# Scores of the global rows: eight heads of a batch as one block of eight tiles, in four PSUM banks

## The chip, the cores and the metric

The kernel runs on one core of one Trainium2 chip. The metric is device time in microseconds of one execution; the kernel before takes 904.69 us (median of three runs).

## What is computed

Two steps: attention of 8 batches with 8 heads each, and then a feed-forward layer on its output. Each head has 512 local rows and 32 global rows of 64 elements. A global row attends to all 544 keys; a local row attends to the 32 global keys and to the local keys at most 32 positions away.

```python
s_g = scale * np.matmul(q_g, k_all.transpose(0, 1, 3, 2))      # k_all: 32 global + 512 local keys
out_g = np.matmul(sm(s_g), v_all)
s_ll = np.where(mask, scale * np.matmul(q_l, k_l.transpose(0, 1, 3, 2)), -1000000000.0)
s_l = np.concatenate([s_lg, s_ll], axis=-1)                    # s_lg: local rows, global keys
out_l = np.matmul(sm(s_l), np.concatenate([v_g, v_l], axis=2))
attn_out = np.concatenate([out_g, out_l], axis=2)
x = attn_out.transpose(0, 2, 1, 3).reshape(B * S, H * D)       # 4352 x 512
h = x @ w_in                                                   # 512 x 2048
g = h * erf(np.maximum(h, 0.0) + np.log1p(np.exp(-np.abs(h))))
out = g @ w_out
```

## The kernel before

**Local rows.** The keys of a head lie in 24 blocks of 32, some of them twice, so that each of 16 windows of 32 rows finds its keys in 128 columns. `attention` (line 451) does one head: q and k come for a pair of heads (64 partitions each), va and vb (the values, one row of them all ones, which gives the softmax sum) for each head. A *run of window scores* (tile `s`) is a pair of heads: 32 small matmuls in the program, 64 rows by 32 columns of the array each, 128 columns wide; in fp32 each is two matmuls in the trace. VectorE masks them and takes the maximum (`sm`, `mx`), ScalarE takes the exponentials, TensorE transposes (`t`), a copy brings them to SBUF (`pt`), and TensorE multiplies with the values (`o`: 128 rows by 32 columns of the array). VectorE divides by the sum (`rs`, `xn`), and the result goes to DRAM by way of a transposed tile (`xT`).

**Global rows.** Four heads are a group. `global_scores` (line 675) computes their scores with four small matmuls of 480 columns into one PSUM bank (`ga`) and four of 64 columns into another (`gb`); head hh uses rows 64 x (hh mod 2) and columns 32 x hh of the array. Then come maximum (`gm`, `gn`), exponentials into the one tile `pg`, six transposes (`gt`), and the values (`go`: 24 matmuls in the program, 48 in the trace), which read the va tiles of the four heads. `global_rows` (line 753) normalizes, and a matmul with a selection matrix (`gx`) brings two heads into place. From batch 5 on (`GSJOIN`) a group's scores are one step with a run of window scores, from batch 6 on (`GOJOIN`) `go` is one step with a pair of `o`.

**Feed-forward.** `x` is split into two parts (`xh`, `xl`), as the weights are, and every product is three matmuls. During the attention the first three eighths of the hidden layer are computed (`h`, the gate, then `op`) for the batches that are done, between the attention's steps. Behind the attention the other five eighths follow, with fewer products by sums of blocks (`pa` to `pd`). TensorE's work is thus of three kinds: full matmuls (`h`, `op`, the transposes, `gx`), score tiles (`s`, `ga`, `gb`) and value tiles (`o`, `go`).

**What sets the order.** Each step is put on a list with `add` (line 131): the engines that may run it, a time to run, a key and what it reads and writes. `schedule` (line 173) plays the list through in the host program and always takes the ready step with the lowest key, if its buffers are free. The keys come from the table of numbers at the top (lines 28 to 78: `HKEYS`, `HOFF` and so on). `NEAR` is how far a step of TensorE's present kind may come ahead of its key; `EVADE`, `CROWD` and `STRETCH` hold back steps of many small instructions. The instructions of each engine then run in that order; all loads and stores are issued on SyncE's queue. `psum_a` has six banks for `s`, `t`, `o`, `ga`, `gb`, `gt`, `go`, `gx` and `op`, a second pool has two for `h`. Until the first `h`, matmuls on constants (`spare`) fill TensorE's planned gaps.

Of the kernel before, what the change touches and what calls it, by code (L numbers as in the profile page):

```python
# [29 lines left out]
CROWD, STRETCH, EVADE = 254, 4.013, 0.302  # L30
# [5 lines left out]
HKEYS = ((0, -4.808), (11, -0.938), (22, 0.485), (64, 33.202))  # L36
STEP, GKEY = 0.082, -0.59
QLEAD, VLEAD, RLEAD, XLEAD = 0.802, -1.384, -3.274, 5.136
GOFF, POFF = 6.111, 3.439
WIN, WOUT = (1.692, -0.833, -2.539), (5.372, 5.751, 6.572)  # L40
BIASED, AG = 28, 3
SHARED = (-99.0, 10.395)
TPAIR = 3.723
KEEP, KSTEP, FIRST = 25.717, 1.786, (18.732, 17.811)
CVO = (54.239, 54.957, 78.914, 61.099, 65.318)
QLEAD2, XDEL, SLOTS = 2.849, -2.014, 11
GATE1, GATE2, PROJ1, PROJ2 = (18.529, 22.625, 24.302), (22.055, 24.328, 43.477), 16.064, 32.464
# [19 lines left out]
WLEAD = 2.131  # L67
LATER, GFIRST = 8, (-3.104, -5.093)
HOFF = (-0.552, -0.319, 0.052, -0.145, -0.077, -0.13, 0.035, -0.016, -0.005, -0.046, 0.01, -0.049, -0.013, 1.49, 2.105, -0.254, 0.767, 0.207, -0.21, 0.858, 0.388, -0.382, 1.584, -2.479, 0.129, -0.149, -0.895, 0.741, 3.078, -0.931, 2.609, 4.711)
XOFF = (-1.743, 3.531, 4.132, 6.479, -2.355, 1.289, 6.274, -1.424, -2.0)  # L70
UOFF = (2.693, -0.229, -0.111, -0.488, 10.393, -2.037, 0.678, -8.495, 2.152)
GFF = (-0.013, 0.75, -1.267, 1.697, -1.821, -1.427, -1.715, -1.652, -1.918)
PFF = (0.156, 0.123, 0.319, 0.471, 0.761, 2.958, 1.452, 0.32, -1.362)
KQ = (2.677, 1.804, -0.704, -0.365, 4.117, -1.317, 9.687, 0.998, 2.585, -6.754)
NORMAL = 1.125 * 2.0**-15
STRAIGHT, XLATE = True, -4.089
# [264 lines left out]
def kernel(  # L341
# [68 lines left out]
    cs = attn.tile([P, 512 + P + 64 + 2], F32, name="cs")  # L410
# [40 lines left out]
    def attention(b, h, key):  # L451
        nm = f"{b}_{h}"
        p, r0 = h // 2, (h % 2) * D
        if h % 2 == 0:
            st["q"] = Q = abuf([P, SQ], f"q_{nm}", "q", 2)
            st["k"] = K = abuf([P, NENT * WB], f"k_{nm}", "k", 2)
            load(key - QLEAD, Q, qT[b, p], 278)
            load(key - QLEAD, K, kE[b, p], 393)
# [7 lines left out]
        st["va", h % 4] = VA  # L466

        biased = NH * b + h < BIASED
        if h % 2 == 0:
# [16 lines left out]
            if h % 4 == 2 and b >= GSJOIN:  # L486
                GA, GB, more = global_scores(b, h // 4, [st["qk", 0], (Q, K)])
                G0[b, h // 4] = GA, GB
# [5 lines left out]
                add({"PE": 1.9}, key, joint, [*st["qk", 0], Q, K], [*SS, GA, GB, GTURN], heat=3136, ins=160, mode="S")  # L494
# [110 lines left out]
        if h % 4 == 3 and not joined:  # L605
# [147 lines left out]
    def global_rows(b, j, O, key):  # L753
        nm = f"{b}_{j}"
        RS = abuf([P, 1], f"gr_{nm}", "gr", 2)

        def norm():
            dve.tensor_scalar(RS.ap, O.ap[:, D : D + 1], 1e-9, None, op0=ALU.add)
            dve.reciprocal(RS.ap, RS.ap)
            dve.tensor_scalar(HALF.ap, half, RS.ap, None, op0=ALU.mult)  # L760
# [642 lines left out]
def _layout(q_l, k_l, v_l, q_g, k_g, v_g, moe_w_in, moe_w_out):  # L1403
# [60 lines left out]
```

## Time and profile before

| | |
|---|---|
| median of 3 runs | 904.69 us (904.61 to 908.22) |
| profiled execution: time | 904.46 us |
| profiled execution: span | 902.7 us |
| mean granted clock of TensorE | 0.996 of full speed |
| instructions in the span | 22276 |
| TensorE busy | 885.5 us |
| VectorE busy | 682.9 us |
| ScalarE busy | 543.7 us |
| GpSimd busy | 12.1 us |
| moved by DMA | 188.22 MB, mean 209 GB/s |

The span is the time from the first to the last instruction of the profiled execution; its own time is a little longer. TensorE has two rows in the profile: PE is its matmuls, PEld its loads of weights, which run beside them. A matmul's row lasts longer than the step from one matmul to the next, because matmuls overlap in the array; what a run costs is read from its start to the start of the run behind it.

### The profile page before, as it was taken

How to read it: one execution, taken by the hardware profiler on the slowest of the kernel's cores; microseconds unless marked ns; L12 is line 12 of the kernel's file. 1: busy time of each engine (PE TensorE's matmuls, PEld its weight loads, DVE VectorE, ACT ScalarE, POOL GpSimd, SP SyncE). 2: the span in 40 equal slices, each digit the busy share in tenths (PEclk: the TensorE clock that was granted, in tenths of full speed). 3: DMA queues.
4: the chain of work that ended last, by engine and by line, in shares of the span. 5: the costliest groups of instructions: out<-in, count | busy, mean ns of one | idle time of the engine just before them, and what ended most of it. 6: DMA issues, size and time to landing. Idle time of an engine off the chain costs nothing.

```text
span 902.7 us, 22276 instructions
## 1 busy us (share of the span) xinstructions
PE 885.5 (98%) x8807; PEld 721.2 (80%) x8807; DVE 682.9 (76%) x1821; ACT 543.7 (60%) x912; POOL 12.1 (1%) x13
## 2 busy tenths in 40 slices
PE   8789999999999999999999999999999999999998
PEld 5567787888878888888888888888888888888886
DVE  6798999969997899987898686487736965465553
ACT  5667977736673796657645583565517571553850
POOL 0002100000000000000000000000000000000000
PEclk9899999999999999999999999999999999999999
DMA  9878886888769958377499836644366426436013
GB/s 337 305 231 286 263 266 211 242 269 278 241 217 299 318 177 292 125 273 274 168 297 369 278 95 192 225 117 129 110 171 211 150 86 195 139 108 213 19 48 117
DMA packets 110016, 188.22 MB, mean 209 GB/s; under 512 B 15576, under 2 KB 39384, under 8 KB 109912
## 3 DMA queue, kind: packets, MB, share of 16 engines
q1 hardware_dynamic: 109912, 186.79, 63.7%
q8 instruction: 70, 1.15, 0.5%
q14 instruction: 34, 0.28, 0.1%
HBM read 145.59 MB, written 41.16 MB: 207 GB/s over the span
## 4 chain that ended last, share of the span: by engine, by line
PE 89%; DMA 5%; DVE 2%; ACT 2%; issue 1%; SPq 1%; DVEq 0%; ACTq 0%
PE op L379 40%; PE h L379 13%; PE pd L379 6%; PE pc L379 6%; PE pa L379 6%; PE o L379 3%; PE pb L379 3%; PE s L379 3%; PE t L380 3%; PE h_g L379 2%; PE ga L379 1%; DMA vb<-in_vB_dram 1%; PE go L379 1%; SPq L383 1%; PE gt L380 1%
## 5 line engine op out<-in xcount | busy, mean ns | idle before, releaser
L379 PE MATMUL op<-wouth,gh 128*128 128x512 f32 x544 | 215.8, 397 | 0.0
L379 PE MATMUL op<-wouth,gl 128*128 128x512 f32 x544 | 212.1, 390 | 0.0
L379 PE MATMUL op<-woutl,gh 128*128 128x512 f32 x544 | 212.0, 390 | 0.0
L382 ACT ACT_TABLE_LOAD x108 | 138.6, 1283 | 2.6 <-PEq L1451 0.7
L379 PEld LDWEIGHTS op<-wouth,gl 128*128 128x128 f32 x544 | 102.1, 188 | 21.8
L379 PEld LDWEIGHTS op<-wouth,gh 128*128 128x128 f32 x544 | 102.2, 188 | 21.5 <-issue 0.6
L379 PEld LDWEIGHTS op<-woutl,gh 128*128 128x128 f32 x544 | 102.3, 188 | 19.5
L381 ACT ACTIVATE gh<-sp 128x512 fp32r<-128x512 f32 x65 | 40.2, 629 | 104.9 <-PE op L379 88.8
L391 DVE TENSOR_TENSOR gl<-sp,gh 128x512 fp32r<-128x512 f32 x134 | 90.4, 689 | 12.8 <-PE op L379 9.3
L379 PE MATMUL h<-xh,winh 128*128 128x512 f32 (+1 forms) x216 | 85.2, 395 | 0.0
L379 PE MATMUL h<-xh,winl 128*128 128x512 f32 (+1 forms) x216 | 81.9, 379 | 0.0
L379 PE MATMUL h<-xl,winh 128*128 128x512 f32 (+1 forms) x216 | 81.7, 378 | 0.0
L381 ACT ACTIVATE sp<-sp 128x512 f32<-128x512 f32 x136 | 75.9, 622 | 0.5
L391 DVE CUSTOM_DVE_ANT_0 sm<-s,cs 128x128 f32<-128x128 f32 x256 | 57.6, 285 | 15.4 <-PE s L379 8.3
L391 DVE CAST gh<-sp 128x512 fp32r<-128x512 f32 x71 | 29.2, 422 | 36.0 <-PE op L379 35.8
L379 PE MATMUL pd<-xh_T,wq 128*128 128x512 f32 x160 | 55.6, 389 | 0.0
L379 PE MATMUL pa<-xh_B,wq 128*128 128x512 f32 x160 | 55.6, 389 | 0.0
L379 PEld LDWEIGHTS h<-xh,winh 128*128 128x128 f32 x216 | 40.6, 188 | 9.8 <-issue 2.2
L379 PEld LDWEIGHTS h<-xh,winl 128*128 128x128 f32 x216 | 40.6, 188 | 8.0
L391 DVE TENSOR_TENSOR pair<-u,pc 128x512 f32<-128x512 f32 x40 | 27.4, 685 | 24.8 <-PE pc L379 24.5
L379 PEld LDWEIGHTS h<-xl,winh 128*128 128x128 f32 x216 | 40.7, 189 | 6.7
L379 PE MATMUL o<-vb,pt 128*32 128x65 f32 x1280 | 37.7, 221 | 7.0 <-issue 5.1
(160 smaller groups left out, 1640.3 us busy)
## 6 DMA issues: line engine op xcount, KB each, us to landing
wq<-wq SPq DMA_DIRECT2D x140, 256.0 KB, 3.0
vb<-in_vB_dram SPq DMA_DIRECT2D x64, 325.0 KB, 5.6
rx<-xsc SPq DMA_DIRECT2D x30, 512.0 KB, 5.5
va<-in_vA_dram SPq DMA_DIRECT2D x64, 195.0 KB, 5.4
k<-in_kE_dram SPq DMA_DIRECT2D x32, 384.0 KB, 5.0
wq<-part SPq DMA_DIRECT2D x35, 256.0 KB, 5.0
q<-in_qT_dram SPq DMA_DIRECT2D x32, 272.0 KB, 4.5
part<-os SPq DMA_DIRECT2D x34, 256.0 KB, 4.6
```

The lines of the kernel that those rows point to most:

```text
L379: pe = lambda n, *a, **k: pinned(nc.tensor.matmul(n, *a, **k))
L380: tr = lambda *a, **k: pinned(nc.tensor.transpose(*a, **k))
L381: act = lambda *a, **k: pinned(nc.scalar.activation(*a, **k))
L382: table = lambda name: pinned(nc.scalar.preload_act_table_set(name))
L383: dma = lambda *a, **k: pinned(nc.sync.dma_start(*a, **k))
L391: return lambda *a, **k: pinned(f(*a, **k))
```

## The change

From batch 1 on (`WHOLE`) `whole_scores` takes the place of two calls of `global_scores`. It issues the scores of all eight heads as one *block*: the eight `ga` matmuls in the order half 0, half 1 for each of the four column places, then the eight `gb` matmuls. The second half takes its heads with their neighbours swapped (`n ^ j`), so that it uses the other 64 rows at each column place. The block has two `ga` and two `gb` banks. In batches 1 to 4 it is a step of its own behind head 7, in batches 5 to 7 one step with the window scores of heads 6 and 7. The softmax and the values of each half are as before, but both come behind the block; `go` is no longer one step with `o`. The swap is taken back by a third column of the `half` mask. q and k tiles are held in rings of four, va in one of seven, vb in one of three (the plan counts on two of them, as before). The numbers that set the order are all different.

```diff
-CROWD, STRETCH, EVADE = 254, 4.013, 0.302
+CROWD, STRETCH, EVADE = 254, 4.013, 0.92
...
-HKEYS = ((0, -4.808), (11, -0.938), (22, 0.485), (64, 33.202))
+HKEYS = ((0, -4.835), (11, -0.96), (22, 0.654), (64, 33.085))
...
-MORE = {"vb": 2}
+MORE = {"vb": 1}
...
-NEAR = 7.126
+NEAR = 0.48
...
+WHOLE, KBUFS, QBUFS, VBUFS = 1, 4, 4, 7
+G2KEY = 0.438
...
-EARLY |= {"k_0_6": ("k3", 0), "q_0_6": ("q3", 0)}
...
-            st["q"] = Q = abuf([P, SQ], f"q_{nm}", "q", 2)
-            st["k"] = K = abuf([P, NENT * WB], f"k_{nm}", "k", 2)
+            st["q"] = Q = abuf([P, SQ], f"q_{nm}", "q", QBUFS)
+            st["k"] = K = abuf([P, NENT * WB], f"k_{nm}", "k", KBUFS)
...
-        VA = abuf([P, NENT // 4, D + 1], f"va_{nm}", "va", 5)
-        VB = abuf([P, NWIN - 6, D + 1], f"vb_{nm}", "vb", 4)
+        VA = abuf([P, NENT // 4, D + 1], f"va_{nm}", "va", VBUFS)
+        VB = abuf([P, NWIN - 6, D + 1], f"vb_{nm}", "vb", 3)
...
-            if h % 4 == 2 and b >= GSJOIN:
-                GA, GB, more = global_scores(b, h // 4, [st["qk", 0], (Q, K)])
-                G0[b, h // 4] = GA, GB
+            if h == 6 and b >= GSJOIN:
+                GA, more = whole_scores(b, [st["qk", n] for n in range(4)])
...
-                add({"PE": 1.9}, key, joint, [*st["qk", 0], Q, K], [*SS, GA, GB, GTURN], heat=3136, ins=160, mode="S")
+                add({"PE": 2.05}, key, joint, [x for n in range(4) for x in st["qk", n]], [*SS, *GA, GTURN], heat=4200, ins=192, mode="S")
...
-        if h % 4 == 3 and b >= GOJOIN:
+        if h % 4 == 3 and WHOLE > b >= GOJOIN:
...
-        if h % 4 == 3 and not joined:
+        if b >= WHOLE:
+            if h == 7:
+                if b < GSJOIN:
+                    GA, scores = whole_scores(b, [st["qk", n] for n in range(4)])
+                    add({"PE": 1.05}, key + GKEY, scores, [x for n in range(4) for x in st["qk", n]], [*GA, GTURN], heat=2176, ins=64, mode="S")
+                for j in range(2):
+                    attention_global(b, j, [st["va", 4 * j + (i ^ j)] for i in range(4)], None, key + GKEY + G2KEY * j)
+        elif h % 4 == 3 and not joined:
...
+    def whole_scores(b, qk):
+        GA = [psum_a([P, 480], f"ga_{b}_{j}") for j in range(2)]
+        GB = [psum_a([P, 64], f"gb_{b}_{j}") for j in range(2)]
+        G0[b, 0], G0[b, 1] = zip(GA, GB)
+
+        def scores():
+            for T, k0 in ((GA, None), (GB, 672)):
+                for n in range(4):
+                    for j in range(2):
+                        hh = n ^ j
+                        Q, K = qk[2 * j + hh // 2]
+                        r0 = (hh % 2) * D
+                        kk = K.ap[r0 : r0 + D]
+                        kk = kk[:, k0 : k0 + 64] if k0 else kk[:, 64:704].rearrange("p (m x) -> p m x", x=P)[:, :, 0:96]
+                        pe(T[j].ap[WB * n : WB * n + WB, :], Q.ap[r0 : r0 + D, :SG], kk, start=True, stop=True)
+
+        return [*GA, *GB], scores
```

What this does to the order is seen at three places. In the names behind a kind the first number is the batch and the next the head (for `ga`, `gb` and `go` the half of the heads, for `s` the pair's first head and then which of the two); the last is a running number.

TensorE in batch 5, before, around its first group. The second group stands in the same way behind the window scores of heads 6 and 7, some 220 rows further on.

```order
L379 MATMUL s_5_2_1_4107<-k_5_2_3797,q_5_2_3788 32x128 x4
L379 MATMUL ga_5_0_4108<-k_5_0_3779,q_5_0_3776 32x480 x2
L379 MATMUL ga_5_0_4108<-k_5_2_3797,q_5_2_3788 32x480 x2
L379 MATMUL gb_5_0_4109<-k_5_0_3779,q_5_0_3776 32x64 x2
L379 MATMUL gb_5_0_4109<-k_5_2_3797,q_5_2_3788 32x64 x2
L379 MATMUL op_0_1_1_3691<-wouth_0_2_2087,gh_0_1_4_3498 128x512
```

The same in the change, where both halves are one block (six more `gb` rows follow):

```order
L380 MATMUL s_5_6_1_4496<-k_5_6_3938,q_5_6_3936 32x128 x4
L380 MATMUL ga_5_0_4497<-k_5_0_3907,q_5_0_3895 32x480
L380 MATMUL ga_5_1_4498<-k_5_4_4015,q_5_4_3978 32x480
L380 MATMUL ga_5_0_4497<-k_5_0_3907,q_5_0_3895 32x480
L380 MATMUL ga_5_1_4498<-k_5_4_4015,q_5_4_3978 32x480
L380 MATMUL ga_5_0_4497<-k_5_2_3928,q_5_2_3913 32x480
L380 MATMUL ga_5_1_4498<-k_5_6_3938,q_5_6_3936 32x480
L380 MATMUL ga_5_0_4497<-k_5_2_3928,q_5_2_3913 32x480
L380 MATMUL ga_5_1_4498<-k_5_6_3938,q_5_6_3936 32x480
L380 MATMUL gb_5_0_4499<-k_5_0_3907,q_5_0_3895 32x64
L380 MATMUL gb_5_1_4500<-k_5_4_4015,q_5_4_3978 32x64
```

The first group has moved behind the scores of heads 6 and 7, and the two halves alternate.

TensorE at the start of the program, before: between the global values of batch 0's first half and the values of heads 5 and 6 stand two filler matmuls.

```order
L379 MATMUL go_0_0_780<-va_0_3_409,gt_0_0_590 32x65
L379 LDWEIGHTS const-bfloat16-1.0
L379 MATMUL spare_77<-const-bfloat16-1.0 128x512
L379 LDWEIGHTS const-bfloat16-1.0
L379 MATMUL spare_77<-const-bfloat16-1.0 128x512
L379 MATMUL o_0_5_819<-va_0_5_567,pt_0_5_596 32x65
```

In the change window scores of batch 1 follow these global values, and values of a head of batch 1 the scores, with no full matmul between them:

```order
L380 MATMUL go_0_0_905<-va_0_3_372,gt_0_0_664 32x65
L380 MATMUL s_1_0_0_938<-k_1_0_486,q_1_0_478 32x128 x4
L380 MATMUL s_1_0_1_939<-k_1_0_486,q_1_0_478 32x128 x4
L380 MATMUL s_1_0_0_938<-k_1_0_486,q_1_0_478 32x128 x4
L380 MATMUL s_1_0_1_939<-k_1_0_486,q_1_0_478 32x128 x4
L380 MATMUL s_1_0_0_938<-k_1_0_486,q_1_0_478 32x128 x4
L380 MATMUL s_1_0_1_939<-k_1_0_486,q_1_0_478 32x128 x4
L380 MATMUL s_1_0_0_938<-k_1_0_486,q_1_0_478 32x128 x4
L380 MATMUL s_1_0_1_939<-k_1_0_486,q_1_0_478 32x128 x4
L380 MATMUL o_1_5_984<-va_1_5_814,pt_1_5_629 32x65
```

Three kinds of work that stood apart are now one stretch of small tiles.

SyncE's queue in batch 6, before, at the load of the last va tile; `waits PE_49` is a wait for TensorE, here for the values that last read the tile's place.

```order
L383 DMA vb_6_4_5609<-in_vB_dram 128x650 [waits DMAHW3_49,PE_49]
L383 DMA va_6_5_5611<-in_vA_dram 128x390 [waits DMAHW4_49,PE_49]
L383 DMA vb_6_5_5619<-in_vB_dram 128x650 [waits DMAHW5_49]
L383 DMA va_6_6_5625<-in_vA_dram 128x390 [waits DMAHW6_49,PE_49]
L383 DMA va_6_7_5634<-in_vA_dram 128x390 [waits DMAHW7_49,PE_49]
```

In the change the va tiles of heads 5 and 6 stand some 50 rows further up, and the last one stands alone behind q and k of batch 7:

```order
L384 DMA q_7_6_5904<-in_qT_dram 128x544 [waits DMAHW6_49,PE_49]
L384 DMA k_7_6_5909<-in_kE_dram 128x768 [waits DMAHW7_49]
L384 DMA q_7_4_5932<-in_qT_dram 128x544 [waits DMAHW0_49,PE_49]
L384 DMA k_7_4_5938<-in_kE_dram 128x768 [waits DMAHW1_49]
L384 DMA va_6_7_6133<-in_vA_dram 128x390 [waits DMAHW2_49,PE_49]
L384 DMA va_7_2_6137<-in_vA_dram 128x390 [waits DMAHW3_49,PE_49]
```

It waits for the global values of batch 6's first half, and the next ones on TensorE that are not full matmuls, the global values of the second half, read it.

## Rows read from the trace of the kernel before

**Rows 1.** The page: busy time of each engine, and the chain that ended last

```profile
PE 885.5 (98%) x8807; PEld 721.2 (80%) x8807; DVE 682.9 (76%) x1821; ACT 543.7 (60%) x912; POOL 12.1 (1%) x13
...
PE 89%; DMA 5%; DVE 2%; ACT 2%; issue 1%; SPq 1%; DVEq 0%; ACTq 0%
```

**Rows 2.** Four stretches: us, then each engine's busy time, clock, DMA share, GB/s

```profile
0.00:48.00 48.00, 39.30 (x857) 26.23 (x865) 34.12 (x152) 29.83 (x79) 3.50 (x7) 0.93 0.88 315
48.00:160.00 112.00, 107.14 (x2261) 84.11 (x2248) 101.89 (x406) 86.22 (x185) 8.63 (x6) 1.00 0.80 252
160.00:373.00 213.00, 213.00 (x3299) 171.91 (x3284) 190.28 (x655) 140.32 (x231) 0.00 (x0) 1.00 0.78 251
373.00:903.00 530.00, 526.11 (x2440) 438.98 (x2428) 356.56 (x611) 287.29 (x420) 0.00 (x0) 1.00 0.54 173
```

**Rows 3.** TensorE's waits, whole span: total us, times, longest us

```profile
PE o L379 <- issue: 5.1, 3, 4.0
PE o L379 <- DMA vb<-in_vB_dram: 1.8, 1, 1.8
PE s L379 <- DVE mx L391: 1.5, 1, 1.5
```

**Rows 4.** Timeline of TensorE: start us, us, instruction; starts of three neighbouring runs

```profile
105.34 1.16 PE L379 MATMUL s<-k,q 64*32 64x128 f32 x64
106.43 0.50 PE L379 MATMUL h<-xh,winh 128*128 128x512 f32 x1
...
109.40 0.24 PE L379 MATMUL o<-va,pt 128*32 128x65 f32 x1
```

**Rows 5.** The same, a run of window scores with a group behind it

```profile
115.13 1.16 PE L379 MATMUL s<-k,q 64*32 64x128 f32 x64
116.03 1.06 PE L379 MATMUL ga<-k,q 64*32 64x480 f32 x8
116.83 0.37 PE L379 MATMUL gb<-k,q 64*32 64x64 f32 x8
117.13 0.50 PE L379 MATMUL op<-wouth,gh 128*128 128x512 f32 x1
```

**Rows 6.** Tile ga: weight loads, ns min/median/max

```profile
L379 PEld LDWEIGHTS ga<-k,q x128: 102/106/107, 9.4 to 359.2; 64*32 64x32 f32 x128
```

**Rows 7.** Chain of waits in order of time: one long run of full matmuls

```profile
859.64 36.76 PE op L379 x162
```

**Rows 8.** Timeline of TensorE: values of two heads, then of one head

```profile
121.45 0.24 PE L379 MATMUL o<-va,pt 128*32 128x65 f32 x1
...
122.50 0.55 PE L380 MATMUL gt<-cs,pg 128*128 128x128 f32 x3
...
44.96 0.24 PE L379 MATMUL o<-va,pt 128*32 128x65 f32 x1
...
45.56 0.66 PE L380 MATMUL t<-cs,sm 128*128 128x128 f32 x4
```

**Rows 9.** Loads of va in the whole span, 28 to 42 us, 300 to 373 us: median us

```profile
va<-in_vA_dram SPq DMA_DIRECT2D x64, 195.0 KB, 5.4
...
va<-in_vA_dram SPq DMA_DIRECT2D x5, 195.0 KB, 7.3
...
va<-in_vA_dram SPq DMA_DIRECT2D x7, 195.0 KB, 3.2
```

**Rows 10.** The stall at 35.87 us: TensorE's timeline, a stretch, instruction fetches

```profile
33.22 0.90 PE L379 MATMUL go<-va,gt 128*32 128x65 f32 x48
...
39.84 0.27 PE L379 MATMUL o<-vb,pt 128*32 128x65 f32 x1 [3.97 <-issue]
...
41.41 1.53 PE L379 MATMUL go<-va,gt 128*32 128x65 f32 x48
...
39.84:45.00 5.16, 5.16 (x74) 3.89 (x75) 3.66 (x12) 1.95 (x6) 0.00 (x0) 0.53 0.32 112
...
q8 instruction: 70, 1.15, 0.5%
```

More of the change, by code (lines that the diff above doesn't have):

```diff
@@ L34 @@
 SPARE = 120.0
-HKEYS = ((0, -4.808), (11, -0.938), (22, 0.485), (64, 33.202))
[L37 to L40, printed above, removed]
-BIASED, AG = 28, 3
[L42 to L47, printed above, removed]
+HKEYS = ((0, -4.835), (11, -0.96), (22, 0.654), (64, 33.085))
+STEP, GKEY = 0.122, -0.629
+QLEAD, VLEAD, RLEAD, XLEAD = 0.935, -1.064, -2.908, 3.698
+GOFF, POFF = 6.905, 4.408
+WIN, WOUT = (-0.309, -0.408, -3.438), (2.119, 4.657, 9.953)
+BIASED, AG = 28, 3
+SHARED = (-99.0, 7.427)
+TPAIR = 2.06
+KEEP, KSTEP, FIRST = 21.87, 2.133, (22.617, 23.563)
+CVO = (73.099, 74.646, 65.836, 59.938, 61.255)
+QLEAD2, XDEL, SLOTS = -2.557, -5.835, 11
+GATE1, GATE2, PROJ1, PROJ2 = (20.074, 24.467, 17.355), (22.987, 24.073, 26.911), 17.046, 28.47
 SPT = 0.35
-BIAS, AHEAD = 1.579, 13.005
-MORE = {"vb": 2}
+BIAS, AHEAD = 1.659, 11.96
+MORE = {"vb": 1}
 SLACK, PORT = {"PE": 0.8, "SP": 0.8}, 1.0
 TURN = {"FS": 0.11, "FO": 0.11, "SF": 0.35, "OF": 0.28, "SO": 0.31, "OS": 0.30}
-NEAR = 7.126
+NEAR = 0.48
 PAIRED, GOJOIN, GSJOIN, PTS = 16, 6, 5, 4
 SMS, SPARED = 4, 0
+WHOLE, KBUFS, QBUFS, VBUFS = 1, 4, 4, 7
+G2KEY = 0.438
 EARLY = {f"{n}_0_{2 * p}": (f"o{x}{p}", 0) for n, x in (("k", "h"), ("q", "l")) for p in range(FIRSTU)}
-EARLY |= {"k_0_6": ("k3", 0), "q_0_6": ("q3", 0)}
 EARLY |= {f"va_0_{h}": ("hs" if h < 4 else "sp", 6 if h < 4 else 6) for h in range(8)}
@@ L66 @@
 EARLY |= {f"vb_0_{h}": ("xh" if h % 2 == 0 else "xl", 3) for h in range(6)}
[L67 to L74, printed above, removed]
+WLEAD = 1.776
+LATER, GFIRST = 8, (-1.585, -5.782)
+HOFF = (-0.025, -0.724, -0.211, -0.06, -0.209, -0.989, -2.398, -0.827, 0.005, -0.086, -0.213, 0.249, 0.176, -0.554, -0.398, 0.03, 1.263, -2.121, -0.737, -1.027, -0.783, -0.436, 2.437, -0.065, 0.129, -0.483, -1.12, -1.594, 6.061, 1.786, 6.584, 3.401)
+XOFF = (16.003, -1.541, 2.959, -3.01, 2.001, -6.37, 3.34, 3.743, -4.694)
+UOFF = (-0.766, -3.006, -3.24, -1.598, 4.562, 1.75, -3.126, -0.753, -3.885)
+GFF = (1.448, 0.484, -1.53, -7.127, -0.598, -1.392, -7.052, -7.271, 4.186)
+PFF = (-2.8, -1.814, 7.755, -1.52, 0.098, 1.367, -0.044, 6.208, -4.799)
+KQ = (7.546, -7.32, -2.605, -7.638, 12.94, -4.993, -6.443, 6.504, 16.598, -6.06)
 NORMAL = 1.125 * 2.0**-15
-STRAIGHT, XLATE = True, -4.089
+STRAIGHT, XLATE = True, -8.002
 SET_EXP = "exp_and_others"
@@ L408, in load @@
         add({"SP": SPT}, key, lambda: dma(dst.ap, src), reads=deps, writes=[dst, *also], moved=kbytes)
-    cs = attn.tile([P, 512 + P + 64 + 2], F32, name="cs")
+    cs = attn.tile([P, 512 + P + 64 + 3], F32, name="cs")
     CS = fixed(cs)
@@ L551, in values @@
                 )
-        group = b, h // 4, [st["va", i] for i in range(h % 4 + 1)], [st["qk", i] for i in range(h % 4 // 2 + 1)]
+        h0 = h // 4 * 4
+        group = b, h // 4, [st["va", i] for i in range(h0, h + 1)], [st["qk", i] for i in range(h0 // 2, p + 1)]
         joined = None
-        if h % 4 == 3 and b >= GOJOIN:
+        if h % 4 == 3 and WHOLE > b >= GOJOIN:
             joined = global_probs(*group, key + GKEY)
@@ L754, in global_rows @@
         nm = f"{b}_{j}"
+        swap = j if b >= WHOLE else 0
         RS = abuf([P, 1], f"gr_{nm}", "gr", 2)
@@ L759, in norm @@
             dve.reciprocal(RS.ap, RS.ap)
-            dve.tensor_scalar(HALF.ap, half, RS.ap, None, op0=ALU.mult)
+            dve.tensor_scalar(HALF.ap, half[:, swap : swap + 2], RS.ap, None, op0=ALU.mult)
         def spread(e):
@@ L1422, in _layout @@
     wo = np.ascontiguousarray(moe_w_out).view(np.int64).reshape(8, 2, P, 512)
-    cst = np.zeros((P, 512 + P + 64 + 2), np.float32)
+    cst = np.zeros((P, 512 + P + 64 + 3), np.float32)
     i, j = np.arange(WB)[:, None], np.arange(WB)[None, :]
```

8 lines of the change are left out of this document (4 added, 4 removed).

## The prediction

> **What bounds the kernel now.** I read the page first, then the stretches, then TensorE's waits, then single runs of matmuls. The page says that TensorE is busy for 98% of the span and is 89% of the chain that ended last [rows 1]. The stretches say where the other 2% lie: 8.7 us of the first 48 us are idle (48.00 less 39.30), 4.9 us of the next 112 us, nothing at all between 160 and 373 us, where the attention ends, and only the tail behind that [rows 2]. So from 160 us on every microsecond that leaves TensorE's stream leaves the span, while before that the time can also be lost or won in waits. The waits name them: 5.1 us of "issue" in three pieces (TensorE waited for nothing but its own instructions), 1.8 us for a load of vb, 1.5 us for VectorE [rows 3]. VectorE is second: 91% busy from 48 to 160 us and 89% from 160 to 373 us [rows 2]. It has room, but little.
>
> **What one group costs.** With starts read against starts, a run of window scores alone takes 106.43 - 105.34 = 1.09 us [rows 4]; the same run with one group of four heads behind it takes 117.13 - 115.13 = 2.00 us [rows 5]. One group costs 0.91 us, a batch's two groups 1.83 us. What does that time hold? Eight ga matmuls, two to a tile (the program issues four, the trace shows eight), and the gb matmuls begin 0.80 us after the first ga: two passes of 0.40 us, so the four tiles ran side by side. They fill half of the array: four of the eight tiles of 64 rows by 32 columns. That eight run together is seen in the window scores: they are 64 matmuls of 128 columns, and at 0.40 us for 480 columns one takes 0.107 us; 64 of them would need 1.71 us four at a time and 0.86 us eight at a time. The run takes 1.09 us [rows 4].
>
> **The change, part by part.**
> *The block.* In batches 1 to 7 the second group moves into the idle half of the array. If all eight tiles run together the block costs what one group cost, 0.91 us, and at most a little skew: the second four tiles need their weights first, and one load takes 0.106 us [rows 6]. I take 1.02 us. The bounds are 0.91 us and 1.83 us (no overlap). Saved: 7 x (1.83 - 1.02) = **5.7 us**, between 6.4 and 0. Batch 0 keeps its two groups, and no matmul is added or dropped.
>
> *Switches between full matmuls and small tiles.* I counted runs in TensorE's order: 71 of full matmuls, 32 of scores, 40 of values before; 68, 37 and 43 in the change. A run has a fixed cost. Twelve full matmuls take 109.40 - 106.43 = 2.97 us [rows 4] and twelve steps of a long run 12 x 36.76/162 = 2.72 us [rows 7]: 0.25 us. Two heads of values take 122.50 - 121.45 = 1.05 us and one takes 0.60 us [rows 8]: 2 x 0.60 - 1.05 = 0.15 us a run. For a run of scores no pair of rows gives it; it lies between 0.15 and 0.25, I take 0.20. So 5 x 0.20 + 3 x 0.15 - 3 x 0.25 = **+0.7 us**, between 0.4 and 1.0.
>
> *The ring of seven va tiles.* A va tile is now held until its half's global values are done, and these come only after the block at head 6 or 7. Seven tiles hold heads 0 to 6, so the eighth va of a batch can be loaded only when the first half's global values have run, and the second half's global values read it. What covers the load is what TensorE does in between: in batch 6 twelve op matmuls, ten transposes and a small one, about 4.4 us by the prices above; in the other batches 5 to 7 us. The load lands 5.4 us after issue in the median, 7.3 us between 28 and 42 us, 3.2 us between 300 and 373 us [rows 9]. In batch 6, before 320 us, a load of 3.2 us is covered, and 5.4 us elsewhere just about: I take **+0.3 us** for all; between 0 and 7 x 1.5 us. On SyncE, what is queued behind that load are the next batch's va tiles, which have 12 us or more until their use.
>
> *The start.* On SyncE q and k of batch 1's pair of heads 4 and 5 (656 KB, 2.1 us at the 315 GB/s of this stretch [rows 2]) go ahead of va and vb of head 0, and runs of scores and values stand next to each other 13 times where they did twice. Both meet the largest loss of the old start: 3.97 us of "issue" at 35.87 us, in which the clock fell to its lower level, 1.2 GHz; it is granted 0.53 of full speed until 45 us [rows 10]. The same 48 global-value matmuls take 1.53 us behind it and 0.90 us before it, so the 4.6 us up to 44.96 us cost some 1.9 us more. That is 6 us for one stall. Its cause reads off the instruction fetches: 70 packets for 17,600 TensorE instructions, so one for every 250 [rows 1, 10], and a run of scores or a pair of values is 128 of them within 1.1 us. Nothing in the rows tells whether the new order meets a late fetch at that place: I take **0**, between -6 us (the stall goes) and +12 us (two more like it).
>
> *What costs nothing.* The softmax of the second half waits for the one probability tile, as before; what hides it is TensorE's full matmuls, and VectorE's spare time. Some copies change between ScalarE and VectorE, and four elementwise operations leave GpSimd for VectorE, whose 9 to 11% of idle time hides them; without it they would cost at most what GpSimd took for six, 8.6 us [rows 2]. One more filler matmul stands where TensorE has nothing else. Behind the attention the same matmuls follow without a gap.
>
> **The sum**: 904.46 us of the profiled execution - 5.7 + 0.7 + 0.3 = 899.8 us. That execution lies 0.23 us under the median of the runs shown; the forecast is **899.8 us**, 0.5% faster, which is about the least that a measurement of this kernel can tell from no change.
>
> **The rivals.**
> *A: the stall at the start goes.* For it: the fetch at 35.87 us came while the DMA engines were busy for 88% of the time [rows 2], and 3.97 us is nearly four fifths of all issue waits [rows 3]. Against: the loads of the first 48 us are still the same bytes and the runs stand closer. 899.8 - 6 = 894 us.
>
> *B: late instructions become the bound, on the slower side.* Place: the first 50 us, where runs of scores and values now touch (one go, one score and one value run are 288 instructions in a row; the longest before was 224). Price: 6 us a stall. It decides from an extra 9 us on (4.7 us of gain and the 4.5 us that can be told from no change); two more stalls of that size give 899.8 + 12 = 912 us. The Trainium skill, Runtime: NRT & Kernel Launch, Instruction fetch mechanics, says that fetching is hidden because instructions are dispatched more slowly than they are fetched. By that rule this rival and A would both be void; the trace disagrees, with 3.97 us.
>
> *C: banks and buffers take the gain.* In batches 5 to 7 window scores and block are one step that takes two and four banks, all six of the accumulating pool. TensorE must have had every other result read out first. The cover is a run of twelve full matmuls (2.97 us) or more before the step. The longest wait for VectorE so far is 1.5 us [rows 3]. If it comes at each of the three steps, 4.5 us go: 899.8 + 4.5 = 904.3 us, no change. Late va tiles, 0.6 us in each of seven batches, give as much.
>
> *D: the change doesn't do what it says: the eight tiles do not run together.* Then nothing is saved: 904.46 + 0.7 + 0.3 = 905.5 us. For it: in the block matmuls of the upper and of the lower 64 rows write the same bank at once. Against: a group does so already, and its four tiles take two passes, not four [rows 5]. The Trainium skill, TensorEngine Tiling (Array Packing), Restrictions and Gotchas, says that different row tiles cannot access one PSUM bank at the same time. By that rule the block would gain nothing; here the trace disagrees for four tiles, which write different quarters of the bank, and for eight no run shows it yet.
>
> **How the numbers follow.** Forecast 0.47, A 0.13, B 0.15, C 0.19, D 0.06. The forecast's own spread, from the bounds of block, switches and ring, is 897 to 903 us, and 900.2 us is where "faster" ends; two thirds of it I count as faster. So faster 0.31 + 0.13 = 0.44; within 0.5% 0.16 + 0.19 + 0.06 = 0.41; slower 0.15. The range of 8 in 10 takes A in at the lower end and leaves out the larger half of B: 893.5 to 908.0 us.
>
> **What would show it.** In the changed profile: a block behind a run of window scores ends about 2.1 us after that run's start, and gb begins 0.9 us after ga; the idle time of TensorE beyond 160 us stays under 1 us; "issue" stays near 5 us and the clock falls once, near 35 us. A wait of op or go matmuls for va shows the ring's price, a wait of window scores for VectorE that of the banks. The prediction is wrong if a batch's block takes 1.8 us, if the first 48 us hold more than 12 or less than 5 us of idle time, or if idle time turns up between 160 and 373 us.

## The result, and the profile after

The changed kernel takes 910.64 us (median of 20 runs, 906.2 to 913.5), the kernel before 904.95 us (20 runs, 899.1 to 908.2). The ratio on record is 1.0052, with a 95% interval of 1.0037 to 1.0067; the two medians alone give 1.0063. The change is **0.5% slower**, where 0.5% faster was forecast. The profiled execution took 912.78 us (span 911.0), 2.1 us over its median; the one of before stood 0.5 us under its own. Of the 8.3 us between the two spans some 2.6 us are thus chance.

The page: busy time of each engine, and the chain that ended last [rows 1].

```profile
PE 885.4 (97%) x8799; PEld 720.2 (79%) x8808; DVE 681.5 (75%) x1823; ACT 545.0 (60%) x918; POOL 6.5 (1%) x9
...
PE 86%; DMA 5%; DVE 5%; ACT 2%; issue 2%; SPq 0%; DVEq 0%; ACTq 0%
```

TensorE's busy time is what it was, 885.4 us, though the block takes some 6 us out of it: as the account below shows, the lower clock puts about as much back. DVE has come into the chain (5% after 2%). The four stretches of [rows 2]:

```profile
0.00:48.00 48.00, 36.77 (x743) 24.41 (x751) 34.55 (x153) 26.27 (x67) 3.71 (x7) 0.89 0.88 319
48.00:160.00 112.00, 103.60 (x2098) 80.85 (x2098) 95.20 (x373) 78.62 (x172) 2.78 (x2) 0.97 0.75 236
160.00:373.00 213.00, 210.60 (x3278) 168.74 (x3284) 184.83 (x634) 151.43 (x254) 0.00 (x0) 1.00 0.78 253
373.00:903.00 530.00, 530.00 (x2674) 442.89 (x2659) 364.10 (x660) 288.63 (x426) 0.00 (x0) 1.00 0.54 173
```

Idle are 11.2 us of the first 48 (8.7 before), 8.4 of the next 112 (4.9) and 2.4 up to 373 us (none), and the clock is lower in two stretches. TensorE's waits over the whole span [rows 3]:

```profile
PE o L380 <- issue: 6.8, 3, 3.0
PE o L380 <- DMA vb<-in_vB_dram: 3.8, 4, 2.2
PE s L380 <- DVE top_in L392: 2.0, 1, 2.0
PE t L381 <- ACT sm L382: 1.9, 2, 1.8
```

No single wait stands out: the old ones are longer, and one for ScalarE joins them. **The block itself** does all that was hoped. TensorE's timeline in batch 5, with the next run's first row [rows 5]:

```profile
232.47 1.16 PE L380 MATMUL s<-k,q 64*32 64x128 f32 x64
233.36 1.06 PE L380 MATMUL ga<-k,q 64*32 64x480 f32 x16
234.17 0.37 PE L380 MATMUL gb<-k,q 64*32 64x64 f32 x16
234.47 0.50 PE L380 MATMUL h<-xh,winh 128*128 128x512 f32 x1
```

Window scores and block take 234.47 - 232.47 = 2.00 us, what scores and one group took before. The block costs 2.00 - 1.09 = 0.91 us, and gb begins 0.81 us after ga: eight tiles together are as fast as four.

**The clock.** Four stretches of the changed kernel, in the columns of [rows 2]; before there was one, from 39.84 us on [rows 10].

```profile
34.00:37.40 3.40, 3.18 (x44) 2.05 (x42) 2.81 (x15) 3.06 (x9) 0.43 (x1) 0.52 0.98 330
41.00:47.80 6.80, 5.55 (x26) 3.71 (x28) 5.13 (x24) 2.84 (x7) 0.00 (x0) 0.50 0.39 120
98.90:102.40 3.50, 3.48 (x36) 2.82 (x37) 3.50 (x14) 1.35 (x3) 0.00 (x0) 0.51 1.00 380
140.00:143.40 3.40, 3.40 (x10) 2.63 (x9) 3.26 (x7) 1.79 (x3) 0.00 (x0) 0.50 0.73 169
```

Each is at 1.2 GHz, the lower level, and begins in or behind a gap. Three of the gaps in TensorE's timeline:

```profile
42.03 0.32 PE L380 MATMUL o<-vb,pt 128*32 128x65 f32 x1 [3.05 <-issue]
...
98.92 0.28 PE L380 MATMUL o<-vb,pt 128*32 128x65 f32 x2 [2.23 <-DMA vb<-in_vB_dram]
...
137.68 1.18 PE L381 MATMUL t<-cs,sm 128*128 128x128 f32 x8 [1.75 <-ACT sm L382]
```

Half the speed for 3.18 + 5.55 + 3.48 + 3.40 us of work costs some 7.7 us: 2.8 us in and behind the wait of 3.05 us, and 1.5 to 1.7 us at each of the others. So a wait can cost twice, but not every one does. No lower clock followed the changed kernel's own waits of 2.01 us up to 14.15 us and of 1.75 us up to 54.40 us, nor two longer ones in the runs below: 3.08 us up to 39.71 us in e5 and 3.56 us up to 99.95 us in e18.

**An account.** To part these terms I cut the first 400 us of every profile into pieces of 2 us and summed, for TensorE, 2 - busy (idle) and (1 - granted clock) x busy (clock). "Work" is the span less both: TensorE's time at full clock, with the tail and the warm-up matmuls.

| profile | idle 0-60 | 60-160 | 160-400 | clock | work | span |
|---|---|---|---|---|---|---|
| before | 9.2 | 4.3 | 0.0 | 2.4 | 886.7 | 902.7 |
| after | 13.2 | 6.5 | 2.4 | 7.6 | 881.4 | 911.0 |
| mean of five in the old order (before, e8, e10, e12, e16) | 9.1 | 4.3 | 1.0 | 1.1 | 887.7 | 903.3 |
| mean of eight in the new order (after, e5, e7, e9, e13 to e15, e17) | 12.1 | 6.7 | 2.0 | 4.3 | 882.6 | 907.7 |

The labels are those of the runs below. The work fell by 5.3 us (5.1 in the means); the forecast had 5.7 - 0.7 = 5.0. All of it went, and more, in idle time and clock: 8.5 + 5.1 us between the two profiles, 6.3 + 3.2 us between the means. By stretches the two profiles lost 5.9 us before 60 us (3.9 idle, 2.0 clock), 5.4 us from there to 160 us (2.2 and 3.2) and 2.4 us behind; the means lost 4.3, 4.0 and 1.2 us. What made these is what the runs below look for.

### The profile page after: what moved, and what is told of

Same layout as the page of the kernel before. It is cut to its first block, busy times and chain, and to the rows that moved or that the text cites. A ratio compares the mean times of both kernels' runs of the same rounds, so it can differ in the third digit from the quotient of the medians.

```text
span 911.0 us, 22302 instructions
## 1 busy us (share of the span) xinstructions
PE 885.4 (97%) x8799; PEld 720.2 (79%) x8808; DVE 681.5 (75%) x1823; ACT 545.0 (60%) x918; POOL 6.5 (1%) x9
## 4 chain that ended last, share of the span: by engine, by line
PE 86%; DMA 5%; DVE 5%; ACT 2%; issue 2%; SPq 0%; DVEq 0%; ACTq 0%
PE op L380 39%; PE h L380 14%; PE pd L380 6%; PE pc L380 6%; PE pa L380 6%; PE pb L380 3%; PE s L380 3%; PE o L380 3%; PE t L381 2%; DMA vb<-in_vB_dram 2%; DVE sm L392 2%; PE h_g L380 2%; PE go L380 1%; PE gt L381 1%; DMA raw_out<-in_w_out_dram 1%
## 5 line engine op out<-in xcount | busy, mean ns | idle before, releaser
L382 ACT ACTIVATE gh<-sp 128x512 fp32r<-128x512 f32 x55 | 33.9, 629 | 100.8 <-PE op L380 92.6
L392 DVE CAST gh<-sp 128x512 fp32r<-128x512 f32 x81 | 33.8, 422 | 46.6 <-PE op L380 46.4
L382 ACT ACTIVATE hs<-h 128x512 f32<-128x512 f32 x38 | 22.7, 596 | 34.8 <-PE h L380 34.5
```

The source lines that it names most:

```text
L382: act = lambda *a, **k: pinned(nc.scalar.activation(*a, **k))
L392: return lambda *a, **k: pinned(f(*a, **k))
```

## The experiments

The theory after the result was this: the block gains its 6.4 us, and the new order of the work loses more in waits before 160 us, each with a stretch at the lower clock. Rivals: the block's held buffers and banks lose the time whatever the order; or the start alone does, by late instructions. The kernel before ran again beside every set of runs, with medians of 904.5 to 906.1 us. A ratio is taken within its set; medians of different sets can be set against each other only to within some 1.5 us.

| run | median us (range, runs) | ratio to before, 95% interval |
|---|---|---|
| e1 old numbers, block | 946.93 (943.7 to 950.2, 4) | 1.0457 (1.0415 to 1.0498) |
| e2 block without overlap | 914.12 (912.4 to 916.4, 4) | 1.0098 (1.0070 to 1.0126) |
| e3 NEAR of before | 908.09 (907.0 to 910.2, 7) | 1.0047 (1.0019 to 1.0076) |
| e4 EVADE of before | 923.37 (919.1 to 927.3, 4) | 1.0198 (1.0157 to 1.0238) |
| e5 two vb loads earlier | 910.46 (905.8 to 913.2, 4) | 1.0065 (1.0040 to 1.0090) |
| e6 and softmax earlier | 913.51 (911.3 to 917.1, 4) | 1.0093 (1.0066 to 1.0120) |
| e7 after, 46 more | 905.99 (904.1 to 912.5, 10) | 1.0009 (0.9986 to 1.0033) |
| e8 before, 56 more | 906.23 (903.2 to 909.6, 10) | 1.0010 (0.9995 to 1.0026) |
| e9 after, fewer bytes | 907.63 (905.4 to 910.4, 10) | 1.0027 (1.0005 to 1.0049) |
| e10 before, fewer bytes | 902.46 (899.0 to 908.1, 10) | 0.9976 (0.9954 to 0.9997) |
| e11 block in batches 5 to 7 | 909.77 (908.0 to 915.1, 9) | 1.0064 (1.0041 to 1.0088) |
| e12 before, smaller rings | 903.51 (902.3 to 907.1, 12) | 0.9985 (0.9969 to 1.0001) |
| e13 after, 24 more | 909.60 (905.9 to 917.0, 8) | 1.0038 (1.0022 to 1.0053) |
| e14 after, 92 more | 903.87 (902.3 to 910.1, 10) | 0.9993 (0.9972 to 1.0014) |
| e15 after, 138 more | 909.14 (906.2 to 910.8, 10) | 1.0033 (1.0018 to 1.0048) |
| e16 before, 112 more | 910.06 (908.3 to 911.7, 5) | 1.0045 (1.0028 to 1.0063) |
| e17 after, 68 more | 905.85 (901.1 to 908.4, 12) | 1.0001 (0.9985 to 1.0018) |
| e18 after, 92 more and vb | 905.42 (902.9 to 912.6, 12) | 1.0016 (0.9994 to 1.0038) |

**The block alone (e2).**

```diff
-                        hh = n ^ j
+                        hh = n
...
-                    attention_global(b, j, [st["va", 4 * j + (i ^ j)] for i in range(4)], None, key + GKEY + G2KEY * j)
+                    attention_global(b, j, [st["va", 4 * j + i] for i in range(4)], None, key + GKEY + G2KEY * j)
...
-        swap = j if b >= WHOLE else 0
+        swap = 0
```

> The order of the changed kernel, instruction for instruction, but the two halves of the block use the same four tiles (head n in row half n mod 2 in both), so that a half waits for the other. Theory 1: TensorE pays 0.92 us more in each of seven batches, 910.6 + 6.4 = 917 us, and a block behind window scores lasts 3.0 us in place of 2.07. Theory 2, that TensorE's time in the block is hidden behind other waits: 910.6 to 912 us.

The same place in batch 5 of this run, TensorE's timeline:

```profile
229.47 1.16 PE L380 MATMUL s<-k,q 64*32 64x128 f32 x64
230.36 1.88 PE L380 MATMUL ga<-k,q 64*32 64x480 f32 x16
231.97 0.51 PE L380 MATMUL gb<-k,q 64*32 64x64 f32 x16
232.41 0.50 PE L380 MATMUL h<-xh,winh 128*128 128x512 f32 x1
```

2.94 us in place of 2.00. The order is the same in both, so starts can be set side by side, step by step, and in each of the seven batches this run falls back by 0.92 to 0.94 us over the block. The overlap is worth 7 x 0.93 = 6.5 us of TensorE's time. The median grew by only 3.5 us. Two things are read from the same comparison. Up to the block of batch 1 the two programs are one and the same, and still this execution reaches the go matmuls at 41.60 us where the profiled changed kernel has them at 48.05: chance alone moves the start by 6.5 us. And most of what is lost in the blocks of batches 1 and 2 is won back within two runs, because the wait for vb behind each is shorter: 0.56 us are gone behind the first, and 1.67 us stand in place of 2.23 us behind the second, without the lower clock. From batch 3 on, at 156 us, all of it stays.

**The numbers (e1, e3, e4, e11).** All numbers of the kernel before, or one of them:

```diff
-NEAR = 0.48
+NEAR = 7.126
...
-CROWD, STRETCH, EVADE = 254, 4.013, 0.92
+CROWD, STRETCH, EVADE = 254, 4.013, 0.302
```

> The block of eight tiles under the numbers of the kernel before (its keys, offsets, NEAR 7.126 and EVADE 0.302); only the buffers of q, k, va, vb and gxT are those of the change, and the two extra tiles for q and k of batch 0 go. TensorE's order is the old one up to the global scores of batch 1. Theory 1, the new order loses and the block gains its 6.4 us: 897 to 901 us, idle time of TensorE before 160 us near the 13.6 us of the kernel before, one issue wait of some 4 us near 35 us. Theory 2, the block and its held buffers lose the time whatever the order: 905 to 911 us, with waits for va, vb or for banks between 48 and 373 us.

> The changed kernel with NEAR at 7.126 as before, all other numbers new: runs of scores and values touch 7 times in place of 13. Theory 1 in its form that touching small runs make the issue stalls of the start: issue waits fall from 6.8 us to 4 or less and the time to 904 to 908 us. If the stalls depend on where the runs meet a fetch and not on touching: 908 to 913 us, with as much issue wait.

> The changed kernel with EVADE at 0.302 as before, all other numbers new. TensorE's order is that of the change up to the values of heads 0 and 1 of batch 1, so the first stalls (to about 50 us) must come again: issue waits of 5 to 7 us, half clock in 40 to 50 us. Theory 1: what comes behind is another order and can lose more or less, 905 to 913 us. Theory 2: 909 to 912 us, as the block is the same.

e1 missed both expectations by far. Its stretch from 160 to 373 us, in the columns of [rows 2], has 23 us of idle time and a lower clock:

```profile
160.00:373.00 213.00, 189.97 (x3018) 148.97 (x3017) 154.36 (x568) 118.77 (x197) 0.00 (x0) 0.93 0.65 209
```

The numbers belong to one program: with the block in it, the old ones set an order that is 36 us worse than the new ones. e4 shows the same with one number (12.7 us worse). e3 has a median 2.5 us lower, which its ratio does not tell from the change's (1.0047 against 1.0052). It has no stretch at the lower clock and 1.7 us of issue waits before 60 us, as expected of fewer touching runs. But by the account above it has 10.0 us idle between 60 and 160 us (6.5 without the edit), and 17 more warm-up matmuls where TensorE had nothing to do.

e11 keeps the old numbers and puts the block into batches 5 to 7 only, so that no instruction of TensorE moves before 195 us.

```diff
-WHOLE, KBUFS, QBUFS, VBUFS = 1, 4, 4, 7
+WHOLE, KBUFS, QBUFS, VBUFS = 5, 4, 4, 7
...
-PAIRED, GOJOIN, GSJOIN, PTS = 16, 6, 5, 4
+PAIRED, GOJOIN, GSJOIN, PTS = 16, 6, 8, 4
```

> The numbers of the kernel before, the block only in batches 5 to 7, where TensorE is never idle; TensorE's order is the old one up to the projections of the second expert block near 200 us (buffers: two more tiles for q and k, two for va, one less for vb and gxT). Theory 1 (the block gains 0.92 us a batch where TensorE sets the pace, less its switches: nine more runs at 0.15 to 0.25 us): 904.9 - 2.8 + 1.7 = 903 to 905 us, no idle time of more than 1 us between 160 and 373 us. Rival (held buffers and banks make waits in this stretch): 906 us or more, with idle time of 2 us or more there.

The time is the rival's, the reason is not: of the 5.3 us idle between 160 and 373 us 1.55 and 2.07 us are issue waits, at 184.7 and 312.4 us, and 0.75 us is a wait for DVE; none is for a bank or for va. The wait at 184.7 us even stands where TensorE's order is still the old one. And by the account the work is 888.2 us, 1.5 more than before, though three blocks give 2.8. So something in this order, its nine more runs or another thing, costs some 4 us where 1.7 was expected; which it is stays open.

**Single waits (e5, e6, e12).** Moves in the finished order, with TensorE's queue untouched: SyncE's loads of vb for heads 2 and 3 of batch 2 go forward (e5); with that, ScalarE's softplus chain and VectorE's softmax go ahead of the split of a late raw_out tile (e6, by five more such pairs: 588 to 586, then 588, 591, 593 and 595 to 600).

```diff
-    for op in prog.schedule():
+    line = prog.schedule()
+    for a, z in ((417, 411), (420, 412)):
+        line.insert(z, line.pop(a))
+    for op in line:
```

> The changed kernel with one move in SyncE's queue: the vb loads of heads 2 and 3 of batch 2 go ahead of a va load, a raw_out load and an rx load (three places). Theory 1 (each wait before 160 us costs itself and a stretch at 1.2 GHz behind it): the 2.2 us wait of the values for vb near 97 us goes, and with it the stretch of 3.5 us at the lower clock up to 102.4 us, so 910.6 - 2.2 - 1.7 = 906.7 us; the granted clock from 98 to 104 us is 1.00. Rival (in the first 160 us something behind the wait is late anyway and takes the time back): 909.5 to 911.5 us, with other waits of some 2 to 4 us between 97 and 160 us.

> The same and a second move: on ScalarE the chain of softplus and erf of the first expert block, and on VectorE the softmax of heads 4 and 5 of batch 3, go ahead of the split of one raw_out tile whose load lands late. Theory 1: the waits of TensorE for sm, pt and hs between 136 and 139.9 us (3.3 us idle) go, and the 3.4 us at the lower clock behind them, so 906.7 - 3.3 - 1.7 = 901.7 us. Rival: 908 to 911 us, the time comes back in other waits.

The rival was right both times. In e5 the wait for vb at 97 us is gone, and TensorE's next wait in its place is this one (it keeps the lower clock, too):

```profile
96.64 1.97 PE L381 MATMUL t<-cs,sm 128*128 128x128 f32 x8 [2.35 <-ACT pg L382]
```

What does a transpose of sm want of the exponential that writes pg? Not data: sm was finished by 93.6 us. It starts a fresh PSUM bank. Two of the six hold the values of heads 2 and 3, four hold the block, and the first of those comes free when ScalarE has read it. ScalarE in e5:

```profile
95.93 0.66 ACT L382 ACTIVATE pg<-ga,gn 128x480 f32<-128x480 f32 x1 [1.76 <-DVE gn L392]
```

It waited for DVE, which reached the maxima of ga at 93.59 us, 3.6 us after the block had ended, behind the window maxima and a raw_out tile that landed late. The same wait at the same place is 3.40 us in e6 and 3.56 us in e18. In e6 a second one of 5.09 us (t behind xn) came from the moved split itself.

e12 leaves every queue of the kernel before as it is:

```diff
-MORE = {"vb": 2}
+MORE = {"vb": 1, "gxT": -1}
...
-        VB = abuf([P, NWIN - 6, D + 1], f"vb_{nm}", "vb", 4)
+        VB = abuf([P, NWIN - 6, D + 1], f"vb_{nm}", "vb", 3)
```

> The kernel before, every engine's order unchanged, but with the smaller rings of the change: three tiles for vb in place of four, one for gxT in place of two. Theory 1 (the waits for vb, 3.8 us in the changed kernel and 1.8 us before, come from the smaller ring): 907 to 909 us, with waits of the values for vb of 3 us or more. Rival (they come from where the loads stand in SyncE's queue): 904 to 906 us, waits for vb of 2 us or less.

The rival again: with three vb tiles and one gxT tile the kernel before is not slower (0.9985). Its longest wait for vb is 0.8 us. In the old order the smaller rings cost nothing, so the longer waits for vb go with where the new order puts the loads.

**The start (e7 to e10, e13 to e18).** Fewer bytes: of three raw_in tiles an eighth is loaded.

```diff
-        add({"SP": SPT}, key, lambda: dma(dst.ap, src), reads=deps, writes=[dst, *also], moved=kbytes)
+        few = 64 if (dst.name or "").startswith(("raw_in_0_0_0", "raw_in_0_1")) else None
...
+                pool.memset(dst.ap.bitcast(F32), 0.0)
+            dma(dst.ap[:, :few], src[:, :few]) if few else dma(dst.ap, src)
```

> The changed kernel, order unchanged, but of three raw_in tiles (units 1 and 0) only 64 of 512 columns are loaded, the rest is set to zero on GpSimd: 1.4 MB less of some 15 MB in the first 48 us, most of it at 23 to 27 us (their weights are left out of the result). Theory 1 (fetches of instructions queue behind loads, and each late one costs itself and a stretch at 1.2 GHz): issue waits before 60 us fall from 6.8 to under 3 us, the clock is 1.00 from 34 to 48 us, and 910.6 - 6 = 904 to 906 us. Rival (behind the start other waits take the time back): the stalls go, but 909 to 911 us. If the load of the DMA engines has no part in it: stalls and time stay.

> The same three tiles cut in the kernel before: 0.9 MB less at 15 to 17 us and 0.5 MB less at 31 us. Theory 1: the stall of 4 us near 36 us goes in most executions, 904.9 - 6 = 898 to 900 us. Rival: 903 to 905 us with the stall gone. Together with the cut of the changed kernel: whatever is left between the two is not the start; by theory 1 some 5 to 6 us, the waits of the new order between 60 and 160 us.

Both got faster, by 3.0 and 2.5 us, half of what theory 1 said, and the profile of e10 holds no wait over 1.3 us before 60 us and no stretch at the lower clock. In e9 the issue waits before 60 us fall from 6.8 to 3.8 us, but one of 3.17 us stays, up to 47.69 us, with some 5.6 us at the lower clock behind it, against the sign that was set for it. This fits late instructions that hang on the loads, though it does not show it alone: other loads land earlier, too. And the two kernels gained about the same by it: 5.2 us are still between them.

The place of the fetches: the first warm-up matmuls are cut into pieces, so that the same work has more instructions.

```diff
-    prog.filler(0.22, lambda: pe(spare, warm[:, :P], warm, start=True, stop=True), 512, SINCE, SPARE)
+    fills = [0]
+    def warmer():
+        fills[0] += 1
+        n = 2 if fills[0] <= 23 else 1
+        for i in range(n):
+            c = slice(512 // n * i, 512 // n * (i + 1))
+            pe(spare[:, c], warm[:, :P], warm[:, c], start=True, stop=True)
+    prog.filler(0.22, warmer, 512, SINCE, SPARE)
```

> The changed kernel, its first 23 warm-up matmuls cut into two halves each: 46 more TensorE instructions before 15 us, no more work, so that each instruction fetch meets the stream at another place. If the issue stalls come where a fetch boundary falls in a stretch with many small matmuls: by counting instructions from fetch to fetch the new places leave less time (3.4 us in place of 5.2 at the sixth fetch, 4.9 in place of 6.4 at the second), so more issue waits, 8 to 12 us, and 912 to 917 us. If the stalls only follow the load of the DMA engines: 909 to 912 us, as before the cut.

> The kernel before, its first 28 warm-up matmuls cut into two halves each: 56 more TensorE instructions before 14 us. If fetch boundaries decide: the new places leave more time (5.8 to 6.9 us in place of 4.3 at the sixth fetch, 6.9 to 8 in place of 5.4 at the third), so the stall of 4 us near 36 us goes or shrinks in most executions: 898 to 902 us. If they do not: 904 to 906 us.

Both expectations missed: 4.6 us faster where slower was worked out, and no difference where faster was. So my count from fetch to fetch does not tell good places from bad ones. Whether the place matters had still to be shown.

> The changed kernel, the first 12 warm-up matmuls in two halves: 24 more TensorE instructions (a weight load and a matmul each) before 5 us. If the place at which a fetch boundary meets the stream decides over the issue stalls, the three counts of this set (24, 92, 138) and the 46 of the run before (906.0 us) differ among each other by 3 us or more, and the idle time before 60 us moves with the time (12 to 13 us in the kernels of this order so far). If any cut of the warm-up gives the 4.6 us: 905 to 907 us here too. If the 906.0 was chance: 909 to 911 us.

> The first 23 warm-up matmuls in three pieces: 92 more instructions before 13 us. By place: another time than with 24, 46 or 138 more, within 903 to 914 us. By any cut: 905 to 907 us. By chance: 909 to 911 us.

> The first 23 warm-up matmuls in four pieces: 138 more instructions before 13 us, the first window scores up to 1 us later. By place: another time than with 24, 46 or 92 more, within 903 to 914 us. By any cut: 905 to 907 us. By chance: 909 to 912 us.

> The kernel before, its first 28 warm-up matmuls in three pieces: 112 more instructions before 14 us (56 more gave 906.2 us, none 904.9). By place: 2 us or more away from 904.9. Otherwise 904 to 906 us.

> The changed kernel with the first 17 warm-up matmuls in three pieces: 68 more instructions, between the two fastest counts so far (46: 906.0 us, 92: 903.9 us). If the place decides and changes smoothly between them: 903 to 907 us. If the counts have no order: anything from 903 to 911 us.

> The changed kernel with 92 more instructions (903.9 us) and with the two vb loads of batch 2 moved ahead as in the fifth run, a try at a version that beats both kernels. If the wait for vb near 95 us is worth its own time here: 902 to 903 us. If, as in the fifth run, the next wait takes it back: 903 to 905 us.

By place: with 0, 24, 46, 68, 92 and 138 more instructions the changed kernel takes 910.6, 909.6, 906.0, 905.9, 903.9 and 909.1 us; the kernel before with 0, 56 and 112 more 905.0, 906.2 and 910.1 us. The counts 0 and 24 lie together, and so do 46, 68 and 92; between 24 and 46 the time falls by 3.6 us, and behind 92 it rises by 5.3. The idle time before 60 us does not move with the time, as it was expected to (9.8 us in e15, 12.6 in e17). With the loss by the clock there it does: 10.6, 12.6, 13.2, 15.6, 17.6 and 18.4 us in e14, e17, e15, e7, the changed kernel and e13, for spans of 902.0, 904.0, 908.9, 910.7, 911.0 and 915.2 us. e14 is the best of the new order; TensorE's waits in its first 60 us, where the changed kernel has 6.8 us of issue:

```profile
PE t L381 <- ACT sm L382: 3.0, 2, 2.5
PE o L380 <- issue: 2.2, 2, 2.0
PE go L380 <- issue: 1.0, 1, 1.0
```

That it is the place, and not only that the start has shifted, is seen in the weight loads. The second count of a row is TensorE's weight loads since the start; with each goes a matmul. Here are stretches that end inside a long issue wait, of the kernel before (which goes on at 39.84 us), the changed kernel (42.03), e2 (45.28) and e7 (48.00), in the columns of [rows 2]:

```profile
0.00:39.80 39.80, 31.23 (x722) 19.80 (x723) 27.85 (x133) 25.48 (x68) 3.50 (x7) 0.98 0.96 349
0.00:42.00 42.00, 31.02 (x716) 20.62 (x723) 29.37 (x129) 23.44 (x60) 3.71 (x7) 0.95 0.94 345
0.00:45.20 45.20, 36.49 (x849) 23.46 (x850) 34.38 (x153) 29.51 (x75) 3.71 (x7) 1.00 0.97 356
0.00:47.90 47.90, 36.56 (x842) 26.92 (x850) 34.65 (x153) 29.48 (x75) 3.72 (x7) 0.96 0.91 332
```

Two different programs stand still behind load 723, and two behind load 850, though e7 has 23 more warm-up loads in front, so that other work stands there. The changed kernel's other two issue waits come behind loads 597 and 977; e7 has one more behind 597, e14 one behind 977. Each step is 126 or 127 loads, with their matmuls some 253 instructions, about the 250 that the prediction read for one fetch (70 packets for 17,600 instructions, [rows 10]). In front of each of the changed kernel's three waits one such packet runs (31.3 to 32.3, 39.8 to 40.8 and 52.0 to 52.9 us) and ends 1.2 to 1.5 us before TensorE goes on. So these waits stand where a fetch falls due, and a few instructions more put other work there. Some waits called issue are not of this kind: 2.04 us of e14's second line, at 18.92 us, come behind load 299. With 12, 23 and 34 more loads in place of its 46 this wait comes behind loads 265, 276 and 287, so it stays with its work.

Averaged over these few places, the change takes 907.5 us and the kernel before 907.1 us. Of the 5.7 us between the medians 3.1 are then a bad place in the one and 2.1 a good place in the other, and 0.4 us are left for the change itself. With six places and three, each scattering by 2.7 us, that rest has a standard error of 1.9 us. The thirteen profiles of the account put it higher, 907.7 - 903.3 = 4.4 us, but they are single executions: by the medians of the same thirteen kernels it is 907.9 - 905.4 = 2.5 us. So it is known only as something between a gain of some 3 us and a loss of some 4 us. e18, the try for a version that beats both, took the vb wait out of e14 and won nothing (905.4 us); the bank wait was there, 3.56 us. Apart from e10, which leaves weights out, no version here is faster than the kernel before by more than its interval.

## Why the prediction was wrong

**Right.** The block: 0.91 us against 1.02, its lower bound; saved 6.4 us. The switches: work fell by 5.3 us, so they and all else cost 1.1 us where 0.7 was taken (bounds 0.4 to 1.0, so just outside). The ring of va: no wait for va in the profile of the change; in the others at most 0.7 us, but 2.3 us once, in e7. Rival D is refuted. The Trainium skill, TensorEngine Tiling (Array Packing), Restrictions and Gotchas, says that different row tiles cannot access one PSUM bank at the same time; by that the eight tiles would have had to take turns. The trace disagrees, with 0.91 us for eight against 0.91 us for four.

**The step that failed is "The start", taken at 0**, and with it the sentence that the second half's softmax is covered: the sum had no term for waits behind the start. In the two profiles the start cost 5.9 us more than before, the time from 60 to 160 us 5.4 us and the time behind it 2.4 us (in the means 4.3, 4.0 and 1.2 us).

The start was priced by one stall, and the sum took the stall of the one profile as a fixed part of the kernel. It is neither fixed nor the order's own: it depends on where the fetches meet the stream, which any edit in front shifts. Three issue waits of 1.97, 3.05 and 1.75 us stood where there had been one of 3.97 and short ones. Rival B had the place of this part, and late instructions as its cause. That its 912 us lies near the 910.6 measured is luck, since it counts 12 us in the first 50 us, where 5.9 were lost before 60 us. And its condition does not hold: the touching of small runs is not what decides, since e13, e14, e15 and e17 touch as often as the change and range over 5.7 us. The Trainium skill, Runtime: NRT & Kernel Launch, Instruction fetch mechanics, says that fetching is hidden, because instructions are dispatched more slowly than they are fetched; the trace disagrees, with 6.8 us in three waits where a fetch falls due.

The rest lies behind the start. Every profile of the new order in the table has more idle time between 60 and 160 us than any of the old one (5.9 us or more against 5.5 or less; 2.4 us more in the means). What stands behind 160 us (1.0 us more idle) and the clock (3.2 us more) hold in the means alone: e5, e14 and e17 lost less by the clock than the kernel before. I had said that idle time beyond 160 us stays under 1 us (it was 2.4) and that the clock falls once (it fell four times). Rival C had the mechanism, four banks held by the block, but looked for it at the joint steps of batches 5 to 7, where no such wait is seen. It bites in batch 2, where VectorE is late with the maxima: 2.35 to 3.56 us as soon as the wait in front of it is taken away. That a wait hides the next one is why e5, e6 and e18 gained nothing.

What stays open: which of the waits between 60 and 160 us would be left in an order fitted to the block, whether such an order keeps the 5 us, and what tells a good place of the fetches from a bad one ahead of a run. Two probability tiles, or maxima earlier on VectorE, were not tried.

## What to carry to other kernels

Where a program's order is fitted to one set of instructions, price an edit of its numbers by what it does to the waits, not by the work that it saves: the work came out within 0.3 us, the waits and the clock cost over 9 us. Before a half-percent change is called a loss or a gain, shift the instruction stream by a few harmless instructions and look at both kernels again; here that alone moves the medians of either by 5 to 7 us (4 to 5 us by the ratios). Behind a gap of 2 us or more look at the clock as well: where it fell, that cost another 1.5 to 2.8 us, but behind some gaps it did not fall.

## What the hardware showed that I had not expected

- Instructions that do no work move the time: 92 more warm-up instructions make the changed kernel 6.7 us faster, 112 more make the kernel before 5.1 us slower. The long waits for instructions stand behind the same counts of weight loads (597, 723, 850, 977) in kernels that have different work there.
- Two executions of the same instruction stream differ by 6.5 us at 48 us, before anything in the two programs differs.
- 1.4 MB less to load in the first 48 us gives 3.0 us in one kernel and 2.5 us in the other, while TensorE's queue is the same.
- A gap of 1.75 us up to 137.68 us, with 0.66 us more up to 139.51 us, had 3.4 us at 1.2 GHz behind it; one of 3.56 us in e18 had none.
